# Putting the first chunk's residual into PSUM through TensorE, with ScalarE copying the sums out

## Chip, cores and metric

The kernel runs on one core of one Trainium2 chip. The metric is the device time of one execution in microseconds (us).

## The reference

Two layers, each a spectral mixing layer (A) and a feed-forward layer (B), both with a layer norm ahead and a residual addition behind:

```python
x = x + _A_ref(_layernorm(x, axis=-1), A_w_r, A_w_i)   # rfft2, times a filter, irfft2, to bf16
x = x + _B_ref(_layernorm(x, axis=-1), B_w1, B_b1, B_w2)
x = x + _A_ref(_layernorm(x, axis=-1), A_w_r, A_w_i)
x = x + _B_ref(_layernorm(x, axis=-1), B_w1, B_b1, B_w2)
# x: 1 x 2048 x 1024 bf16; B: 1024 -> 3584, h * tanh(softplus(h)), 3584 -> 1024
```

What matters here is the seam from A to B. It comes twice, near 110 and near 600 us.

## The kernel before

The residual stream lives in SBUF as `XS`, 16 tiles of 128 rows by 1024. At the seam the last stage of the inverse transform (`i4`) multiplies rows that come back from a round trip through HBM. The first chunk (tiles 0 to 3) is done in four quarters of 32 small products with 32 columns each; each quarter fills two PSUM banks. The other twelve tiles (the "remainder", 96 columns a product) follow in portions of 15 products between other work. While TensorE waits, `spin` gives it products that nobody reads, to keep its clock up.

```python
        self.spin(26, 0)                    # ahead of the wait for rows
# ...
    def i4(self, lo, nb, u0, n, bank):
        # ...
            fns.append(lambda e, l=l: e.matmul(self.PS[:, bank + l // k, l % k * w:(l % k + 1) * w], self.UT.ap[:, u0 + l, :],
                                               self.MT[:, 8 * lo:8 * lo + w], start=True, stop=True))
# ... i4_out, for the first chunk: VectorE adds the PSUM result to XS
                self.op(self.dve, lambda e, src=src, xs=xs: e.tensor_tensor(xs, src, xs, ALU.add), reads=rb, parts=self.r_xs[j])
# ... layer_B; rest(bank) is one portion of the remainder, copied out by ScalarE unless prog says otherwise
        for u in range(4):
            self.i4(0, 4, 32 * u, 32, 2 * u)
            self.i4_out(0, 4, 32 * u, 32, 2 * u, tiles=(0, 2))
            self.i4_out(0, 4, 32 * u, 32, 2 * u, staged=YC, tiles=(2, 2))
            for j in range(2):
                self.stats_quarter(j, u)    # VectorE, layer norm statistics
        rest(0)
        self.root(0, 2)                     # ScalarE square root, then VectorE reciprocal
        rest(3)
        for j in range(2):
            xn[j] = self.apply(j)           # VectorE normalises
        self.spin(6, 7)
        for j in range(2):
            transposed(0, j, xn[j])         # TensorE transposes, VectorE copies back
        rest(3)
        self.warm(ACT.Mish)
        # ... residual, statistics and apply of tiles 2 and 3
        for fg in range(4):
            mm1(0, fg, 0, mid=turns(0, 2, 3) if fg == 3 else ())   # first dense products
            rest(3)
            if fg == 2:
                rest(6, 10, dve)
        mm1(0, 0, 1)
        rest(3, 13)
```

## Time and profile before

| | before |
|---|---|
| time, median of the first three runs | 1017.54 us (1015.78 to 1019.77) |
| profiled execution, first to last instruction | 1016.2 us |
| mean granted TensorE clock of that execution | 0.998 |
| first seam: late rows land (116.31) to transposes (123.68) | 7.37 us |
| second seam: first small product (607.28) to transposes (616.01) | 8.73 us |
| either seam: transposes to first dense product | 2.00 us |
| either seam: first dense product to the gapless dense stretch | 14.56 us |

The last four rows are read off TensorE's line of the timeline. Its columns are start, duration, engine, line, operation, shapes, count, and in brackets how long the engine stood idle before and what ended that. First seam, kernel before:

```profile
116.31 3.21 PE L950 MATMUL PS<-MT,ARENA 128*128 128x32 bf16 x111 [0.94 <-DMA ARENA<-u_scratch]
120.07 0.81 PE L950 MATMUL PS<-MT,ARENA 128*128 128x96 bf16 x15 [0.55 <-ACT ARENA L550]
121.68 1.24 PE L628 MATMUL PS<-FD,BD 128*128 128x512 bf16 x5 [0.79 <-ACT ARENA L550]
123.68 1.08 PE L1006 MATMUL PS<-IDENT,ARENA 128*128 128x128 bf16 x16 [0.76 <-DVE ARENA L512]
...
125.68 1.92 PE L1040 MATMUL PS<-ARENA 128*128 128x256 bf16 x16 [0.29 <-DVE ARENA L1011]
```

The second seam, kernel before:

```profile
607.28 3.48 PE L950 MATMUL PS<-MT,ARENA 128*128 128x32 bf16 x128 [1.58 <-DMA ARENA<-u_scratch]
...
616.01 1.08 PE L1006 MATMUL PS<-IDENT,ARENA 128*128 128x128 bf16 x16 [0.76 <-DVE ARENA L512]
```

No hole of TensorE in the first seam, from the late rows on, is longer than 0.94 us: remainder products and the spin (L628) fill the time that VectorE takes. (The x111 of the first line holds the 96 late small products and the first remainder portion.) "Gapless" is the dense product (L1040) after the last remainder portion, at 140.24: from there on TensorE runs back to back.

### The profile page before, as it was taken

To read this page: it belongs to the slowest core of one execution; us is meant where nothing else is said; L and a number is where in the kernel's file an instruction comes from. 1 tells how busy PE (TensorE), PEld (TensorE's weight loads), DVE (VectorE), ACT (ScalarE), POOL (GpSimd) and SP (SyncE) were. 2 spreads that over 40 slices of the span, in tenths; PEclk is the share of its full clock that TensorE was granted. 3 is DMA by queue.
4 is the path that set the end of the run, shared out by engine and by line. 5 is a ranking of instruction groups with operands and counts; after the bars stand their busy time and mean duration, and the time that the engine had idled before them with its cause. 6 is when DMAs were issued, how large, how long until landed. Compare 5 with 4: busy or idle time off the path is not lost.

```text
span 1016.2 us, 13732 instructions
## 1 busy us (share of the span) xinstructions
PE 955.1 (94%) x5779; PEld 507.3 (50%) x5865; DVE 326.5 (32%) x679; ACT 347.3 (34%) x482; POOL 81.5 (8%) x114
## 2 busy tenths in 40 slices
PE   0799799999999999999999978999999999999998
PEld 0577575444444444444456757644444444444443
DVE  6797469002444000033347736830011100000111
ACT  7798384330000433300029847543100024330000
POOL 4651000000000000002511100000000000000000
PEclk9999999999999999999999999999999999999999
DMA  9979813562111220002932875246411212100000
GB/s 283 247 221 320 212 61 114 181 205 72 47 46 32 73 83 21 1 21 82 195 66 82 233 188 140 89 156 207 126 27 46 73 52 80 45 1 11 21 26 27
DMA packets 154205, 107.00 MB, mean 105 GB/s; under 512 B 74448, under 2 KB 133664, under 8 KB 154144
## 3 DMA queue, kind: packets, MB, share of 16 engines
q1 hardware_dynamic: 143056, 78.61, 27.3%
q0 software_dynamic: 8912, 25.84, 8.8%
q10 hardware_dynamic: 2176, 1.66, 0.5%
q8 instruction: 47, 0.77, 0.3%
q14 instruction: 14, 0.11, 0.0%
HBM read 80.85 MB, written 20.71 MB: 100 GB/s over the span
## 4 chain that ended last, share of the span: by engine, by line
PE 86%; DVE 4%; DMA 4%; ACT 4%; issue 1%; SPq 0%; POOL 0%; ACTq 0%; DVEq 0%; POOLq 0%
PE PS L1057 38%; PE PS L1040 37%; PE PS L771 2%; PE PS L697 2%; PE PS L792 2%; DMA ARENA<-c_bt 1%; PE PS L950 1%; ACT ARENA L441 1%; DMA ARENA<-u_scratch 1%; DVE ARENA L619 1%; DMA XS<-in_A_x_dram 1%; ACT ARENA L550 1%; PE PS L1006 1%; DVE ARENA L592 1%; PE PS L810 1%
## 5 line engine op out<-in xcount | busy, mean ns | idle before, releaser
L1040 PE MATMUL PS<-ARENA 128*128 128x512 bf16 (+1 forms) x1950 | 389.3, 358 | 2.5 <-DVE ARENA L1011 0.6
L1057 PE MATMUL PS<-ARENA 128*128 128x512 bf16 x1756 | 385.5, 379 | 1.9
L1044 ACT ACTIVATE ARENA<-PS,B 128x512 bf16<-128x512 f32 (+1 forms) x248 | 158.9, 645 | 410.9 <-PE PS L1040 410.6
L1040 PEld LDWEIGHTS PS<-ARENA 128*128 128x128 bf16 x1984 | 192.8, 98 | 193.8 <-DVE ARENA L1011 1.5
L1057 PEld LDWEIGHTS PS<-ARENA 128*128 128x128 bf16 x1792 | 175.4, 98 | 211.4
L1062 DVE TENSOR_TENSOR XS<-PS,XS 128x512 bf16<-128x512 f32 x64 | 44.2, 691 | 587.1 <-PE PS L1057 587.1
L460 DVE BATCH_NORM_STATS2 BN<-XS 128x6 f32<-128x512 bf16 x100 | 64.7, 675 | 6.2 <-DMA XS<-in_A_x_dram 5.0
L550 ACT ACTIVATE ARENA<-PS 128x1440 bf16<-128x1440 f32 (+3 forms) x26 | 28.0, 1095 | 28.0 <-DVE XS L972 24.4
L249 POOL DMA_DIRECT2D xn_scratch<-ARENA x12 | 6.5, 541 | 374.5 <-DVE ARENA L512 374.5
L771 PE MATMUL PS<-ARENA 128*128 128x256 bf16 x256 | 32.4, 273 | 4.1 <-DVE ARENA L760 3.2
L778 ACT ACTIVATE ARENA<-PS 128x1024 bf16<-128x1024 f32 x32 | 33.0, 1051 | 7.1 <-PE PS L771 7.1
L432 ACT ACTIVATE RS<-MV,EPS 128x2 f32<-128x2 f32 (+2 forms) x5 | 1.5, 298 | 96.8 <-DVE MV L463 96.2
L697 PE MATMUL PS<-FD,ARENA 128*128 128x256 bf16 (+1 forms) x256 | 31.8, 271 | 2.4 <-ACT ARENA L617 1.2
L749 ACT ACTIVATE ARENA<-PS 128x1024 bf16<-128x1024 f32 x32 | 32.5, 1044 | 4.5 <-PE PS L745 4.5
L771 PEld LDWEIGHTS PS<-ARENA 128*128 128x128 bf16 x256 | 24.2, 98 | 11.8 <-DVE ARENA L760 5.5
L753 DVE TENSOR_TENSOR ARENA<-ARENA 128x1024 bf16<-128x1024 bf16 x32 | 22.0, 688 | 20.4 <-ACT ARENA L749 20.3
L697 PEld LDWEIGHTS PS<-FD,ARENA 128*128 128x128 bf16 x256 | 24.4, 98 | 6.5 <-DVE ARENA L619 1.4
L820 ACT ACTIVATE ARENA<-PS 128x1024 bf16<-128x1024 f32 x26 | 26.7, 1063 | 2.4 <-PE PS L792 2.4
L792 PE MATMUL PS<-ARENA,BD 128*128 128x256 bf16 x192 | 24.9, 273 | 2.3 <-ACT ARENA L778 2.3
L950 PE MATMUL PS<-MT,ARENA 128*128 128x32 bf16 (+1 forms) x512 | 20.9, 195 | 4.5 <-DMA ARENA<-u_scratch 2.5
L512 DVE TENSOR_SCALAR ARENA<-XS,MV,RS 128x1024 bf16<-128x1024 bf16 x48 | 24.8, 542 | 1.0
L732 ACT ACTIVATE ARENA<-PS 128x1024 bf16<-128x1024 f32 x22 | 22.9, 1058 | 3.1 <-PE PS L697 3.1
(76 smaller groups left out, 515.5 us busy)
## 6 DMA issues: line engine op xcount, KB each, us to landing
ARENA<-in_B_w_dram SPq DMA_DIRECT2D x56, 512.0 KB, 3.9
ARENA<-in_B_w_dram SPq DMA_DIRECT2D x56, 256.0 KB, 4.1
u_scratch<-ARENA SPq DMA_DIRECT2D x14, 512.0 KB, 3.7
ARENA<-u_scratch SPq DMA_DIRECT2D x14, 512.0 KB, 6.1
w_scratch<-ARENA POOLq DMA_DIRECT2D x8, 512.0 KB, 6.2
ARENA<-w_scratch POOLq DMA_DIRECT2D x8, 512.0 KB, 5.4
out_dram<-XS SPq DMA_DIRECT2D x16, 256.0 KB, 2.0
ARENA<-xn_scratch POOLq DMA_DIRECT2D x15, 256.0 KB, 10.0
```

The source lines that it names most:

```text
L460: self.op(self.dve, lambda e: e.bn_stats(self.BN[:, j, 6 * h:6 * h + 6], self.XS[:, j, 512 * h:512 * h + 512]), reads=[self.r_xs[j]], part ...
L550: fn = (lambda e: e.activation(dst, src, ACT.Copy)) if scale is None else \
L697: fns.append(lambda e: e.matmul(dst, at(r), FD[:, t:t + n], start=start, stop=stop))
L749: self.op(act, lambda e: e.activation(x.ap.rearrange("p a b -> p (a b)"), ps, ACT.Copy, scale=SIG), reads=banks, writes=[x.res])
L771: fns.append(lambda e, c=c, part=part: e.matmul(ps[:, c * 256:(c + 1) * 256], yk.ap[:, part, c * P:(c + 1) * P], t[:, (128, 0)[part]:(384, ...
L778: self.op(act, lambda e: e.activation(v.ap[:, :, i, :], src, ACT.Copy), reads=banks, parts=[v.res])
L792: fns.append(lambda e, dst=dst, part=part, c=c: e.matmul(dst, BD[:, c:c + P], mov(kd, part), start=(part == 0), stop=(part == 1)))
L950: fns.append(lambda e, l=l: e.matmul(self.PS[:, bank + l // k, l % k * w:(l % k + 1) * w], self.UT.ap[:, u0 + l, :], self.MT[:, 8 * lo:8 * ...
L1040: fns.append(lambda e, db=db, bank=bank, fl=fl: e.matmul(PS[:, bank, 0:w], wb.ap[:, db, fl * P:(fl + 1) * P], x.ap[:, db, tok], start=(db ...
L1044: self.op(act, lambda e, bank=bank, ft=ft: e.activation(at.ap[:, ft, tok], PS[:, bank, 0:w], ACT.Mish, bias=self.B1[:, ft:ft + 1]), reads= ...
L1057: fns.append(lambda e, i=i, ft=ft: e.matmul(PS[:, bank, :], at.ap[:, ft, t * P:(t + 1) * P], W2[ft].ap[:, h * 512:(h + 1) * 512], start=(i ...
L1062: self.op(dve, lambda e: e.tensor_tensor(xs, PS[:, bank, :], xs, ALU.add), reads=[self.r_bank[bank]], writes=[self.r_xs[j]])
```

## The change

The intent is to take the residual addition from VectorE. During the wait for rows, eight identity products write `XS` into PSUM with `start=True`; the small products then accumulate on top; ScalarE copies finished sums out; VectorE only takes statistics. So 18 of 26 spin products go, as do the six behind. The root now stands ahead of the first remainder portion, the third remainder portion no longer stands between the transposes and the first dense product (two precede the transposes, as before), and the remainder's portions for VectorE move (10, 10 and 3 products for one of 10).

```diff
-        self.spin(26, 0)
+        self.spin(8, 0)
+        self.residual_first()
...
+    def residual_first(self):
+        for b in range(8):
+            out = self.PS[:, b, :].rearrange("p (l c) -> p c l", c=32)
+            xs = self.XS[:, 0:4, :].rearrange("p n (h l) -> p (n h) l", l=P)[:, :, 16 * b:16 * b + 16]
+            self.group([lambda e, out=out, xs=xs: e.matmul(out, self.IDENT[:], xs, start=True, stop=False)], ...)
...
-                                               self.MT[:, 8 * lo:8 * lo + w], start=True, stop=True))
+                                               self.MT[:, 8 * lo:8 * lo + w], start=lo > 0,
+                                               stop=lo > 0 or l % k == k - 1))
...
         for u in range(4):
             self.i4(0, 4, 32 * u, 32, 2 * u)
-            self.i4_out(0, 4, 32 * u, 32, 2 * u, tiles=(0, 2))
-            self.i4_out(0, 4, 32 * u, 32, 2 * u, staged=YC, tiles=(2, 2))
+            self.out_first(u, 0, act)
             for j in range(2):
                 self.stats_quarter(j, u)
+        for u in range(4):
+            self.out_first(u, 2, (act, act, act, dve)[u])
+        self.root(0, 2)
         rest(0)
-        self.root(0, 2)
         rest(3)
         for j in range(2):
             xn[j] = self.apply(j)
-        self.spin(6, 7)
         for j in range(2):
             transposed(0, j, xn[j])
-        rest(3)
         self.warm(ACT.Mish)
...
         for j in (2, 3):
-            residual(j)
             self.stats_dve(j)
...
             rest(3)
-            if fg == 2:
-                rest(6, 10, dve)
+            if fg:
+                rest(6, (10, 10, 3)[fg - 1], dve)
         mm1(0, 0, 1)
-        rest(3, 13)
+        rest(3)
```

More of the change, by code (lines that the diff above doesn't have):

```diff
@@ L942, in keep_filter @@
         self.dma(self.pool, self.w_d[g], self.wt_pair(i), f"ws{g % 4}", reads=[w.res for w in self.WT[i:i + 2]], writes=[self.r_wd[g]])
+    def residual_first(self):
+        for b in range(8):
+            out = self.PS[:, b, :].rearrange("p (l c) -> p c l", c=32)
+            xs = self.XS[:, 0:4, :].rearrange("p n (h l) -> p (n h) l", l=P)[:, :, 16 * b:16 * b + 16]
+            self.group([lambda e, out=out, xs=xs: e.matmul(out, self.IDENT[:], xs, start=True, stop=False)],
+                       reads=self.r_xs[0:4] + [self.r_ident], writes=[self.r_bank[b]])
+        for r in self.r_xs[0:4]:
+            r.begin()
     def i4(self, lo, nb, u0, n, bank):
@@ L950, in i4, with out_first, i4_out @@
             fns.append(lambda e, l=l: e.matmul(self.PS[:, bank + l // k, l % k * w:(l % k + 1) * w], self.UT.ap[:, u0 + l, :],
-                                               self.MT[:, 8 * lo:8 * lo + w], start=True, stop=True))
+                                               self.MT[:, 8 * lo:8 * lo + w], start=lo > 0,
+                                               stop=lo > 0 or l % k == k - 1))
         self.group(fns, reads=self.r_ut[u0 // 32:(u0 + n - 1) // 32 + 1] + [self.r_mt], writes=self.r_bank[bank:bank - (-n // k)])
-    def i4_out(self, lo, nb, u0, n, bank, staged=None, prog=None, tiles=None):
+    def out_first(self, u, t, prog):
+        b = slice(2 * u, 2 * u + 2)
+        src = self.PS[:, b, :].rearrange("p b (i c) -> p c b i", c=32)[:, 8 * t:8 * t + 16]
+        dst = self.XS[:, t:t + 2, :].rearrange("p n (h l) -> p (n h) l", l=P)[:, :, 32 * u:32 * u + 32]
+        self.copy(prog, dst.rearrange("p c (b i) -> p c b i", i=16), src, [], self.r_bank[b], parts=self.r_xs[t:t + 2])
+    def i4_out(self, lo, nb, u0, n, bank, staged, prog):
         w = 8 * nb
         k = 512 // w
-        t0, tn = tiles or (0, nb)
         for b0, m, i in ((0, n // k, k), (n // k, 1, n % k)):
@@ L962, in i4_out @@
                 continue
-            src = self.PS[:, bank + b0:bank + b0 + m, 0:i * w].rearrange("p b (i c) -> p c b i", c=w)[:, 8 * t0:8 * (t0 + tn)]
+            src = self.PS[:, bank + b0:bank + b0 + m, 0:i * w].rearrange("p b (i c) -> p c b i", c=w)
             l = slice(u0 + b0 * k, u0 + b0 * k + m * i)
-            rb = self.r_bank[bank + b0:bank + b0 + m]
-            def at(ap):
-                return ap.rearrange("p n (h l) -> p (n h) l", l=P)[:, :, l].rearrange("p c (b i) -> p c b i", i=i)
-            if staged is None:
-                j = slice(lo + t0, lo + t0 + tn)
-                xs = at(self.XS[:, j, :])
-                self.op(self.dve, lambda e, src=src, xs=xs: e.tensor_tensor(xs, src, xs, ALU.add), reads=rb, parts=self.r_xs[j])
-            else:
-                self.copy(prog or self.act, at(staged.ap), src, [], rb, parts=[staged.res])
+            dst = staged.ap.rearrange("p n (h l) -> p (n h) l", l=P)[:, :, l].rearrange("p c (b i) -> p c b i", i=i)
+            self.copy(prog, dst, src, [], self.r_bank[bank + b0:bank + b0 + m], parts=[staged.res])
     def load_w1(self, after=()):
@@ L1092, in layer_B @@
         YS.res.begin()
-        YC = self.alloc("YC", self.ob["XT1"], [2, self.D])
-        YC.res.begin()
         xn = {}
-        for j in range(2):
-            self.r_xs[j].begin()
         def at_tiles(c):
@@ L1114, in residual @@
         def residual(j):
-            y, i = (YS, j - 4) if j > 3 else (YC, j - 2)
-            self.op(dve, lambda e: e.tensor_tensor(self.XS[:, j, :], self.XS[:, j, :], y.ap[:, i, :], ALU.add),
-                    reads=[y.res], writes=[self.r_xs[j]])
+            self.op(dve, lambda e: e.tensor_tensor(self.XS[:, j, :], self.XS[:, j, :], YS.ap[:, j - 4, :], ALU.add),
+                    reads=[YS.res], writes=[self.r_xs[j]])
         def turns(c, *ts):
```

## The prediction

> **What bounds the kernel now.** I read first the page's busy shares, then its chain that ended last, then the chain of work in order of time, then groups by shape and the clock in short windows.
>
> ```profile
> PE 955.1 (94%) x5779; PEld 507.3 (50%) x5865; DVE 326.5 (32%) x679; ACT 347.3 (34%) x482; POOL 81.5 (8%) x114
> ...
> PE 86%; DVE 4%; DMA 4%; ACT 4%; issue 1%; SPq 0%; POOL 0%; ACTq 0%; DVEq 0%; POOLq 0%
> ```
>
> TensorE (PE) carries 86% of the chain that sets the end. The change doesn't touch its dense products (L1040, L1057); all it can win lies in the few per cent where the chain leaves TensorE. One such place comes twice, where each spectral layer ends and the feed-forward layer begins. The chain of work in order of time shows the first, from 107 to 124 us:
>
> ```profile
> 107.34 2.98 DMA u_scratch<-ARENA
> ...
> 111.69 4.58 DMA ARENA<-u_scratch
> 116.27 0.04 issue
> 116.31 0.98 PE PS L950 x32
> 117.30 0.02 issue
> 117.32 0.70 DVE XS L972
> 118.02 0.02 issue
> 118.04 0.75 DVE BN L472 x2
> 118.80 0.60 DVE XS L972
> 119.42 0.75 DVE BN L472 x2
> 120.18 0.60 DVE XS L972
> 120.80 1.86 ACT ARENA L550 x2
> 122.66 0.19 ACT RS L432
> ...
> 123.68 1.08 PE PS L1006 x16
> ```
>
> Columns: start, duration, what. A round trip through HBM (the wait for rows) ends at 116.27; then the small products L950 feed VectorE (DVE), which alternates the residual addition L972 and statistics L472, 1.35 us a turn, till ScalarE (ACT) takes the root and TensorE transposes at 123.68. The second occurrence has the same pieces, but all rows have landed when L950 starts at 607.28, and the transposes start at 616.01. There all four turns are bound by VectorE; in the first only the last three, as the rows of the second quarter came late.
>
> From the groups by shape between 100 and 186 us I take the costs:
>
> ```profile
> L628 PE MATMUL PS<-FD,BD 128*128 128x512 bf16 x30 | 6.8, 379 | 2.3 <-DVE ARENA L818 1.6 <-ACT ARENA L550 0.8
> ...
> L472 DVE BATCH_NORM_STATS2 BN<-XS 128x6 f32<-128x256 bf16 x8 | 3.1, 413 | 0.1
> ...
> L972 DVE TENSOR_TENSOR XS<-PS,XS 128x512 bf16<-128x512 f32 x4 | 2.7, 683 | 7.3 <-PE PS L950 7.3
> L550 ACT ACTIVATE ARENA<-PS 128x512 bf16<-128x512 f32 x4 | 2.4, 597 | 11.7 <-DVE XS L972 11.7
> ```
>
> L628 is the spin (products whose result nobody reads). L550 waited 11.7 us for L972: ScalarE stands idle beside a busy VectorE.
>
> **What the Trainium skill says.** "VectorE: DVE Perf Modes", section "The perf-mode tier table", has a two-tensor operation with a PSUM operand at its lowest rate; the trace agrees: 683 ns for 512 columns, where ScalarE copies the same 512 out in 597 ns. "PSUM — Partial Sum Buffer", section "The four PSUM rules", advises to "put any other seed through the PE (an identity matmul with `first_mm`)", which is what the change does, so accumulation should be right. Its section "Specifications" says that non-contiguous access to PSUM slows matmuls significantly. The new identity products write every 32nd column, so I expect them slower than the spin's; no matmul of the kernel before writes so, thus the trace can't say by how much. "TensorE: Matmul & The Clock Gate", Part 1, has the clock at half after an idle window of about 3.4 us. The trace shows a halving after less: TensorE idled 1.58 us before 607.28, and the windows read
>
> ```profile
> 607.20:608.20 1.00, 0.92 (x37) 0.95 (x38) 0.00 (x0) 0.00 (x0) 0.00 (x0) 1.00 0.42 63
> 608.20:609.20 1.00, 1.00 (x46) 1.00 (x43) 0.90 (x2) 0.20 (x1) 0.00 (x0) 0.78 0.00 0
> 609.20:610.20 1.00, 1.00 (x44) 1.00 (x41) 1.00 (x3) 0.39 (x1) 0.00 (x0) 0.50 0.15 37
> ```
>
> where the clock is the third number from the end. At the first occurrence it stays at 1.00.
>
> **The change part by part.** *During the wait* (108.79 to 114.41, and 600.14 to 607.28): 26 spin products in 5.56 us are 0.21 us each. Eight stay (1.7 us), and eight identity products come. At 0.21 each they take 1.7 us, at twice that 3.4, so that TensorE is done 3.4 to 5.1 us after the start, inside 5.6 and 7.1 us. Cost on the path: none, unless one takes over 0.5 us.
>
> *First occurrence.* Each quarter's L950 takes 0.98 us and the next follows, so the last ends at about 119.2. ScalarE copies tiles 0 and 1 of it by 119.85 (0.60). VectorE then has only the last statistics and aggregates, 1.30 us (120.80 to 122.10 before): 121.2. Before, the last addition ended at 120.77: 0.9 us won. ScalarE meanwhile takes three copies of tiles 2 and 3, each about 0.5 behind the one before: 121.4; the root follows to 121.6. VectorE does its one copy of the fourth quarter, about 0.68 (the 960-column copy takes 1.16, the 1024-column one 1.23, about 1 ns a column), till 121.9, then reciprocal and apply (0.18 and 0.56): transposes at 122.7 for 123.68, so **1.0 us won**.
>
> *Second occurrence.* All products are there (128 in 3.48 us, the last at 610.76). Last copy of tiles 0 and 1 at 611.4, statistics to 612.75 (before 614.43), VectorE's copy to 613.4, transposes at 614.25 for 616.01: **1.75 us won**.
>
> *Then the stretch to dense work* (first L1040 at 125.68 to the gapless stretch from 140.24, 14.56 us). The changed order does two of the twelve-tile remainders (L950, 15 columns each) ahead of the first L1040 instead of three, so the table load (1.28) and the first Mish follow two ScalarE copies of about 1.4 each: Mish can start at 125.85, not 128.51, some 1.1 us after the first L1040 (before 2.8). But 15 more columns fall into the stretch: at 0.043 us each 0.65 us of TensorE. The VectorE loses two additions L1116 (0.66 each) and gets copies of 10, 10 and 3 columns (1.16, 1.16, some 0.46) for one of 10. Replayed in program order with TensorE's start-to-start times (1.75 for 16 products of 256, 0.65 for 15 remainders, 0.9 for 16 transposes), ScalarE's 0.4 for a Mish and 1.4 for a remainder, I get three small stalls of together 0.5 us, against 1.3 before (0.58 at 130.65 for ScalarE, 0.38 at 135.53 for a copy are the largest). TensorE's work there was 5 × 1.75 + 83 × 0.043 + 0.9 = 13.25 us, of the 14.56; it becomes 13.9, and with 0.5 of stalls 14.4: **0.2 us won**. VectorE's first residual additions of tiles 4 to 7 come over a microsecond earlier too; the later stall for L1011 at 157.89 stays.
>
> Sum: (1.0 + 0.2) + (1.75 + 0.2) = 3.15 us, or 1014.4 from 1017.54. Everything after 140.24 is TensorE back to back and moves forward as it is.
>
> **The rivals.**
> *The clock takes the place of the wait.* The change removes 18 spin products ahead and 6 (1.24 us) behind, and with VectorE no longer slow TensorE has holes: at the second occurrence from 610.76 to about 612.5, until ScalarE has freed the banks for the remainder. Against it: the products after the wait ran 27 ns apart at clock 0.50 as at 1.00, so the small ones don't care. For it: remainders of 96 columns, transposes and L1040 do. A half-clock window of 3.4 us over them would cost 1 to 1.7 us at each occurrence; if at both, nothing is left of the gain: 1017 to 1018.
> *The identity products are slow.* At four times 0.21, eight take 6.8 us; with the spin 8.5 against 5.6 and 7.1 available: 1.6 us (first, counted from the second quarter 1.0) and 1.4 lost of the gain, 1016 to 1017. For it stands the skill's sentence; against it, that 18 spin products were taken away for 8, as if each were worth about two.
> *ScalarE becomes the bound.* It had 4.59 us of work in the 9.3 us from 114.3 to 123.6 and now takes all evacuations there but one. But it also takes none of the wait on L972 any more; its last copy ends 0.2 us after the statistics, but VectorE's own copy lasts until 0.3 us after the root and hides that. If the copies took 0.7 rather than 0.6 us, some 0.3 us would be lost each time: 1015.
> *More is won* if the stalls in the stretch vanish: 0.5 each time, 1013.3.
>
> **Range and chances.** I weigh the clock as likely at one of the two places (1 us) and take the prediction to 1015.2, 2.3 us below before. The three times before span 1015.78 to 1019.77, so a median strays by some 1 to 1.5 us by itself. Range 1012.4 to 1018.0. 2% are 20 us; from the landing of the rows to the gapless stretch there are 24 us (116.27 to 140.24) and 25 (607.28 to 632.57), of which TensorE works some 18 each, so at most 13 can be won in all: faster by over 2% gets 1%. Slower by over 2% would need a stall that nothing shows: 1%, and 98% for within.
>
> **What would show each step.** Identity products between 0.21 and 0.43 us apart, done before the first product after the wait. The transposes after apply start about 6.4 us after the late rows land in the first occurrence (before 123.68 − 116.27 = 7.4), and about 7.0 us after the first small product in the second (before 616.01 − 607.28 = 8.7). ScalarE waits for TensorE, no longer for VectorE, at its copies. First dense product (L1040) to the gapless stretch in about 14.4 us. Clock at 1.00 from 122 to 126 and from 612.5 to 616. The prediction is wrong if the small products start later than 5.6 and 7.1 us after the spin's start as before, if the clock reads 0.50 under L1040, or if the span falls by over 5 us.

## The result, and the profile after

| | before | after |
|---|---|---|
| median (range), four runs each | 1016.79 us (1015.78 to 1019.77) | 1015.41 us (1014.96 to 1016.21) |
| ratio, 95% interval | | 0.9982 (0.9959 to 1.0006) |
| profiled execution | 1016.2 us | 1013.1 us |
| its mean clock | 0.998 | 0.995 |

Ratios here are the mean time of one kernel's fast runs over the mean of the other's in the same rounds, so they are not quite the ratio of the medians. The result is correct, and inside 2%. The interval reaches past 1, so the timings alone do not show a gain. From the page after, the busy shares and the shares of the chain that ended last:

```profile
PE 952.0 (94%) x5749; PEld 506.0 (50%) x5833; DVE 323.9 (32%) x673; ACT 348.7 (34%) x484; POOL 81.6 (8%) x114
...
PE 87%; DMA 4%; SPq 3%; DVE 2%; ACT 2%; issue 1%; POOL 0%; ACTq 0%; DVEq 0%
```

TensorE still carries the chain; VectorE's and ScalarE's parts of it each fell from 4% to 2%. About half of each fall lies at the seams (100 to 142 and 590 to 634 us: VectorE 20.0 us of the chain before, 10.4 after; ScalarE 16.8 and 6.3), the other half ahead of 100 us, where nothing was changed. (Of the new 3% put down to a DMA queue, SPq, only some 1.2 us lie in each seam; the rest is elsewhere, where nothing was changed.) Of the 3.1 us between the two profiled executions, 1.6 lie ahead of the changed code: the last evacuation of the spectral layer, which both kernels have, ends at 108.51 before and at 106.90 after. So one may not read 3.1 us as the gain. TensorE's timeline of the first seam, after (L950 is now the identity product, L961 the small and the remainder products, L1016 the transposes, L1050 the first dense product):

```profile
108.92 3.61 PE L950 MATMUL PS<-XS,IDENT 128*128 128x512 bf16 x8
...
114.67 2.68 PE L961 MATMUL PS<-MT,ARENA 128*128 128x32 bf16 x96 [1.36 <-DMA ARENA<-u_scratch]
119.02 2.58 PE L961 MATMUL PS<-MT,ARENA 128*128 128x96 bf16 x30 [1.67 <-ACT XS L550]
121.40 1.40 PE L1016 MATMUL PS<-IDENT,ARENA 128*128 128x128 bf16 x16
123.74 1.92 PE L1050 MATMUL PS<-ARENA 128*128 128x256 bf16 x16 [0.94 <-DVE ARENA L1021]
...
131.94 1.04 PE L1050 MATMUL PS<-ARENA 128*128 128x256 bf16 x8
133.36 1.07 PE L1016 MATMUL PS<-IDENT,ARENA 128*128 128x128 bf16 x16 [0.38 <-DVE ARENA L554]
```

The identity products end before the late rows land (114.67). Transposes start 6.73 us after that, for 7.37. But there is a new hole: between the last small product and the first remainder TensorE is idle for 1.67 us, waiting for ScalarE to empty banks 0 to 2. The timeline of the other engines shows the rest of it:

```profile
117.39 2.06 ACT L550 ACTIVATE XS<-PS 128x512 bf16<-128x512 f32 x4 [0.26 <-PE PS L961]
...
119.37 0.29 ACT L432 ACTIVATE RS<-MV,EPS 128x2 f32<-128x2 f32 x1
...
119.98 1.00 DVE L512 TENSOR_SCALAR ARENA<-XS,MV,RS 128x1024 bf16<-128x1024 bf16 x2
```

ScalarE now follows TensorE, not VectorE. The first normalised tile is ready at about 120.5 (half of the 1.00 us after 119.98), yet its transposes start at 121.40: TensorE is still on the remainder, 30 products in 2.58 us, where the same 30 take 1.45 us in the second seam. The windows say why. Columns: window and length, busy time of TensorE, its weight loads, VectorE, ScalarE, GpSimd, then the granted clock, DMA share and GB/s:

```profile
116.80:117.60 0.80, 0.56 (x21) 0.45 (x17) 0.70 (x3) 0.54 (x2) 0.00 (x0) 0.50 1.00 284
117.60:118.40 0.80, 0.00 (x0) 0.00 (x0) 0.70 (x2) 0.80 (x3) 0.00 (x0) 0.50 1.15 344
...
120.00:120.80 0.80, 0.80 (x14) 0.80 (x12) 0.80 (x2) 0.36 (x1) 0.00 (x0) 0.50 1.12 285
```

The clock reads 0.50 from 115.2 to 122.2: it falls after the wait for rows (1.36 us) and stays down over the new hole. In the second seam of this trace it is at half only from 606.8 to 610.2, under small products; in a repeat it stays there until 614.0. Each first line below is the remainder, each second the transposes, second seam. This is the first trace after:

```profile
611.28 1.45 PE L961 MATMUL PS<-MT,ARENA 128*128 128x96 bf16 x30 [1.67 <-ACT XS L550]
612.84 1.08 PE L1016 MATMUL PS<-IDENT,ARENA 128*128 128x128 bf16 x16
```

and this the repeat (run after_again below):

```profile
611.19 2.58 PE L961 MATMUL PS<-MT,ARENA 128*128 128x96 bf16 x30 [1.67 <-ACT XS L550]
613.57 1.25 PE L1016 MATMUL PS<-IDENT,ARENA 128*128 128x128 bf16 x16
```

The same program lost a good microsecond to the clock in one and nothing in the other. The small products of the second seam after start at 605.73:

```profile
605.73 0.95 PE L961 MATMUL PS<-MT,ARENA 128*128 128x32 bf16 x32 [2.20 <-DMA ARENA<-u_scratch]
606.90 2.72 PE L961 MATMUL PS<-MT,ARENA 128*128 128x32 bf16 x96 [0.22 <-DMA ARENA<-u_scratch]
```

Stretch by stretch, in us from the traces:

| | before | after | after, repeat |
|---|---|---|---|
| 1st seam: late rows to transposes | 7.37 | 6.73 | 6.60 |
| transposes to first dense product | 2.00 | 2.34 | 2.35 |
| first dense product to gapless | 14.56 | 14.54 | 14.54 |
| 2nd seam: first small product to transposes | 8.73 | 7.11 | 7.56 |
| transposes to first dense product | 2.00 | 2.01 | 2.18 |
| first dense product to gapless | 14.56 | 14.54 | 14.54 |
| sum | 49.22 | 47.27 | 47.77 |

That is 1.95 and 1.45 us won, 0.19 and 0.14% of the span; the timed ratios say 0.18 and 0.14%, though with intervals of some ±0.2% that reach past 1.

These stretches leave the wait for rows out. Counted from the spectral layer's last evacuation to the gapless stretch, both seams together, the sums are 64.44 before, 62.86 after and 63.29 in the repeat: 1.58 and 1.15 us won. The difference is the second seam's rows, which landed later: the first small product starts 7.82 and 7.77 us after that evacuation, against 7.42 before. The identity products had ended by then (at 603.5), so they are not what it waited for.

### The profile page after: what moved, and what is told of

Same layout as the page of the kernel before. It is cut to its first block, busy times and chain, and to the rows that moved or that the text cites. A ratio compares the mean times of both kernels' runs of the same rounds, so it can differ in the third digit from the quotient of the medians.

```text
span 1013.1 us, 13670 instructions
## 1 busy us (share of the span) xinstructions
PE 952.0 (94%) x5749; PEld 506.0 (50%) x5833; DVE 323.9 (32%) x673; ACT 348.7 (34%) x484; POOL 81.6 (8%) x114
## 4 chain that ended last, share of the span: by engine, by line
PE 87%; DMA 4%; SPq 3%; DVE 2%; ACT 2%; issue 1%; POOL 0%; ACTq 0%; DVEq 0%
PE PS L1067 38%; PE PS L1050 38%; SPq L249 3%; PE PS L771 2%; PE PS L697 2%; PE PS L792 2%; PE PS L961 2%; DMA ARENA<-in_A_w_i_dram 1%; DMA ARENA<-u_scratch 1%; DMA ARENA<-c_bt 1%; DMA u_scratch<-ARENA 1%; PE PS L1016 1%; PE PS L743 1%; ACT ARENA L778 1%; PE PS L810 1%
## 5 line engine op out<-in xcount | busy, mean ns | idle before, releaser
L1050 PE MATMUL PS<-ARENA 128*128 128x512 bf16 (+1 forms) x1950 | 389.1, 358 | 3.8 <-DVE ARENA L1021 1.9
L1050 PEld LDWEIGHTS PS<-ARENA 128*128 128x128 bf16 x1984 | 193.0, 98 | 194.7 <-DVE ARENA L1021 2.9
L961 PE MATMUL PS<-MT,ARENA 128*128 128x32 bf16 (+1 forms) x512 | 21.4, 199 | 7.1 <-DMA ARENA<-u_scratch 3.8
L961 PEld LDWEIGHTS PS<-MT,ARENA 128*128 128x128 bf16 x512 | 20.0, 102 | 9.8 <-issue 4.5
```

What stands on the lines that cost most here:

```text
L1050: fns.append(lambda e, db=db, bank=bank, fl=fl: e.matmul(PS[:, bank, 0:w], wb.ap[:, db, fl * P:(fl + 1) * P], x.ap[:, db, tok], start=(db ...
```

## The experiments

Theory: the gain is VectorE's relief at the seam, less what the clock takes back where removed spin and new holes drop it. Rival: the gain comes from what else the diff does (root ahead of the remainder, no portion between transposes and first dense product), and VectorE's addition matters little. Edits are against the kernel after unless a line says otherwise.

**A repeat, and the spin ahead of the wait.** The repeat is the kernel after as it is.

> The changed kernel once more, unedited, for a second trace and a tighter ratio. Stretch = from the first spin product after the spectral layer to the first dense product of the gapless stretch (31.45 and 32.43 us in the trace of the kernel before, 31.10 and 31.20 in that of the changed one, so 1.58 us won in sum). Theory (the change wins 1 to 2 us, the rest of the 3.1 us between the two profiled spans came before the changed code): ratio 0.998 to 0.999; stretches within 0.5 us of 31.10 and 31.20 if the clock falls in the same places. Rival (all 3.1 us are the change's): ratio 0.997. If the half-clock time is a matter of a window that doesn't start with the kernel, the mean clock differs between the timed runs (0.993 to 0.996 seen so far) and the place of the half clock differs between the traces.

Ratio 0.9986 (0.9968 to 1.0004), median 1015.77 over six runs (1014.26 to 1020.19). The same size of gain, and again an interval that reaches past 1. Of the two stretches that the expectation names, the first is as said (31.19), the second is not (32.00 for 31.20): the clock fell elsewhere, as seen above.

```diff
-        self.spin(8, 0)
+        self.spin(12, 0)     # spin12;  spin0: line removed
```

> Twelve spin products ahead of the identity products instead of eight: 0.85 us more TensorE work inside the wait. Clock theory (the half clock from 115.4 to 122 us in the changed kernel's first occurrence comes of the holes in TensorE's work that the removed spins left, and costs 0.5 to 1 us there): clock stays at 1.00 in the first occurrence, the 30 remainder products ahead of the transposes take about 1.45 us instead of 2.58, first stretch 30.3 to 30.7 instead of 31.10, ratio to before about 0.9975. Rival (the half clock is chance, or caused by the later hole while ScalarE empties banks): the half clock is there as before and the stretch stays at 31.1.

> No spin products at all ahead of the identity products: 1.7 us less TensorE work inside the wait. Clock theory: half clock in both occurrences, reaching under the remainders and transposes in at least one; stretches (from the first identity product, so 1.7 us shorter by definition; compare by the landing of the rows) lengthen by 0 to 1 us each, mean clock lower than with eight, ratio 0.9985 to 1.000. Rival (spins don't matter): ratio as that of the changed kernel, mean clock as well.

spin12: 0.9981 (0.9966 to 0.9995). spin0: 0.9982 (0.9967 to 0.9996). More spin ahead did not keep the clock (first seam at half from 120.8 to 124.2, second from 609.0 to 615.8), and none at all lowered the mean clock of the runs to 0.990 to 0.995 without costing time. So **the amount of spin ahead of the wait made no difference that these runs can tell** (some ±0.15%). What follows the wait first are small products, which hardly feel the clock: in the second seam before they start 25 ns apart at full clock, up to 608.77, and 27 ns at half.

**How much an identity product costs, and why.** The first variant puts the stride on the read from SBUF instead of on the write to PSUM; the second has no stride at all and computes something else (relative error 0.71). Its output is wrong, which doesn't matter for the time.

```diff
# sbuf_stride
-            out = self.PS[:, b, :].rearrange("p (l c) -> p c l", c=32)
-            xs = self.XS[:, 0:4, :].rearrange("p n (h l) -> p (n h) l", l=P)[:, :, 16 * b:16 * b + 16]
+            out = self.PS[:, b, :].rearrange("p (l c) -> p l c", c=32)
+            xs = self.XS[:, 0:4, :].rearrange("p n (h l) -> p l (n h)", l=P)[:, 16 * b:16 * b + 16, :]
# contig_wrong
+            out = self.PS[:, b, :]
+            xs = self.XS[:, b // 2, 512 * (b % 2):512 * (b % 2) + 512]
```

> The identity products read with the stride (one bf16 every 256 bytes of SBUF) and write PSUM without one; same result. In the changed kernel they are 0.428 us apart, twice the spin's 0.21, with the stride on the writing side. If the PSUM stride is what doubles them, and a strided read costs nothing: 0.21 us apart. If a strided read costs as much: 0.43 again. If the layout is not the cause at all (a wait or weight load for each): 0.43 again with weight loads as late as now, 0.29 us of idle before each. The end moves by nothing either way, as the products end inside the wait for rows.

> Wrong result on purpose: the identity products read and write without a stride. They are 0.428 us apart in the changed kernel with the stride in PSUM, and 0.86 with the stride in SBUF. If strides alone are the cause: 0.21 to 0.22 apart, as the spin. If each product's own wait and signal cost something: more than 0.25. The time is about that of the changed kernel, as the products end inside the wait for rows in all three but the one with the stride in SBUF.

The line of the identity products by itself (minimum, median and maximum of the duration in ns), first of the kernel after, then of sbuf_stride, then of contig_wrong:

```profile
L950 PE MATMUL PS<-XS,IDENT x16: 602/634/634, 108.9 to 602.9; 128*128 128x512 bf16 x16
```

```profile
L950 PE MATMUL PS<-XS,IDENT x16: 1017/1036/1037, 110.9 to 608.7; 128*128 128x512 bf16 x16
```

```profile
L950 PE MATMUL PS<-XS,IDENT x16: 379/379/390, 111.2 to 603.5; 128*128 128x512 bf16 x16
```

Start to start, eight of them are 0.43, 0.86 and 0.22 us apart (for the kernel after: 3.61 less the last one's 0.63, over 7). So the product that writes every 32nd fp32 column of PSUM costs twice a plain one, and the one that reads every 128th bf16 element of SBUF four times. (The first also reads in runs of 16 columns, which contig_wrong changes too; the two were not separated.) sbuf_stride, one run at 1020.86 us, is correct; its identity products end after the rows have landed, and its first small product starts 8.86 us after the spectral layer's last evacuation instead of 5.42. I had expected its end not to move: a miss, as I had not expected the SBUF stride to cost more than the PSUM one.

**Each half of the change alone.** psum_only keeps the residual in PSUM and goes back to the old order of root and portions; order_only keeps VectorE's additions and takes the new order (against the kernel before). Neither has the six spin products.

```diff
# psum_only
-        self.root(0, 2)
         rest(0)
+        self.root(0, 2)
         rest(3)
@@ after the transposes
+        rest(3)
@@ and the tail
-            if fg:
-                rest(6, (10, 10, 3)[fg - 1], dve)
+            if fg == 2:
+                rest(6, 10, dve)
-        rest(3)
+        rest(3, 13)
# order_only, against before
+        self.root(0, 2)
         rest(0)
-        self.root(0, 2)
@@
-        self.spin(6, 7)
@@ after the transposes
-        rest(3)
@@ and the tail as in the kernel after
```

> The residual through PSUM and the copies by ScalarE as changed, but the remainders in the order of the kernel before (three ahead of the table load, VectorE takes ten columns once), the spin ahead of the transposes left out. Theory (the gain comes from VectorE no longer adding): nearly all of the gain is here: transposes 0.7 to 1.2 us earlier than before in each occurrence, from the first dense product to the gapless stretch 14.5 us as before, ratio 0.998 to 0.9985. Rival (the new order of the remainders brings the gain): stretches as before, ratio 1.000.

> The kernel before with only the new order: root ahead of the remainders, two remainders instead of three ahead of the table load, VectorE copies out 10, 10 and 3 columns, no spin ahead of the transposes; the residual still added by VectorE. Times from the end of the last spectral eviction (before: transposes at 15.17 and 16.15, gapless dense products at 31.73 and 32.71). Theory, after the run with the PSUM part alone was 3 us slower: the root waits for statistics alone instead of for a remainder's copy, 0.4 us earlier each time; transposes 14.8 and 15.7, gapless 31.3 and 32.3, ratio 0.9990 to 0.9995, so that about half of the change's gain is the order's and the PSUM part needs the order. Rival (the order is worth nothing without the PSUM part): gapless as before, ratio 1.000. Mean clock 0.998 as before if the holes come of the PSUM part, 0.996 or less if they come of the missing spin ahead of the transposes.

psum_only: 1.0031 (1.0019 to 1.0043), median 1021.05. order_only: 1.0034 (1.0021 to 1.0048), median 1021.25. **Each half alone, without the six spin products, makes the kernel slower**, against my expectations. In psum_only ScalarE, in program order, first copies the remainder and then takes the root for which everybody waits (first seam):

```profile
121.88 1.37 ACT L550 ACTIVATE ARENA<-PS 128x1440 bf16<-128x1440 f32 x1 [0.41 <-PE PS L961]
123.15 0.29 ACT L432 ACTIVATE RS<-MV,EPS 128x2 f32<-128x2 f32 x1
```

The statistics were done near 121.3, so the root is about 1.8 us late; then the half clock lies under transposes and first dense products (123.2 to 130.0; 16 dense products took 3.33 us instead of 1.92). In order_only the order is good, but without the six spin products TensorE stands idle for 2.39 us and meets the dense products at half clock:

```profile
123.61 1.08 PE L1006 MATMUL PS<-IDENT,ARENA 128*128 128x128 bf16 x16 [2.39 <-DVE ARENA L512]
125.61 3.45 PE L1040 MATMUL PS<-ARENA 128*128 128x256 bf16 x16 [0.93 <-DVE ARENA L1011]
```

**Each half again, with spin.** order_spin is order_only with `self.spin(6, 7)` kept. psum_root has the PSUM part, root first, three spin products ahead of the transposes, and otherwise the old order.

```diff
# order_spin, against order_only
+        self.spin(6, 7)
         for j in range(2):
             transposed(0, j, xn[j])
# psum_root, against psum_only
+        self.root(0, 2)
         rest(0)
-        self.root(0, 2)
@@
+        self.spin(3, 7)
         for j in range(2):
             transposed(0, j, xn[j])
```

> The order alone again (residual still added by VectorE), but with the six spin products ahead of the transposes kept. The order alone without them was 0.34% slower at a mean clock of 0.990 to 0.993. Clock theory (the missing spin, not the order, made it slow): half clock no longer under the first dense products, first dense to gapless 14.5 us (without the spin 16.1 and 16.8), from the end of the last spectral eviction transposes at 14.4 to 14.8 and 15.0 to 15.7, mean clock 0.998, ratio 0.9985 to 0.9995. Rival (the order itself, with two more copies by VectorE, makes it slow): ratio 1.002 or more as without.

> The residual through PSUM with the remainders as before (three ahead of the table load, VectorE ten columns once), but the root ahead of the first remainder, and three spin products ahead of the transposes. With the remainder ahead of the root it was 0.31% slower. Theory (there ScalarE's copy of the remainder, 1.4 us, stood between the statistics and the root): root at 12.3 and 13.3 us after the last spectral eviction (not 15.0 and 15.2), transposes at 14.4 and 15.3, gapless at 31.0 to 31.3 and 31.9 to 32.2, ratio 0.998 to 0.999, as the whole change. Rival (two remainders ahead of the table load and the columns for VectorE are needed for the gain): ratio 0.9995 or more.

order_spin: 0.9979 (0.9964 to 0.9993), median 1015.85; clock 0.998 to 1.000 in all five runs. First seam:

```profile
120.62 1.47 PE L628 MATMUL PS<-FD,BD 128*128 128x512 bf16 x6 [0.57 <-ACT ARENA L550]
...
124.44 1.92 PE L1040 MATMUL PS<-ARENA 128*128 128x256 bf16 x16 [0.93 <-DVE ARENA L1011]
```

Six spin products turn order_only's mean of 1021.72 us into 1016.24, and the same 16 dense products take 1.92 us again. So the order with the spin kept, and with **VectorE adding as before**, is by its timing as fast as the whole change. psum_root: 0.9993 (0.998 to 1.0006), median 1017.39: the PSUM part with the root first and otherwise the old order is not told from before. The interval covers both what the theory expected (0.998 to 0.999) and what the rival did, so this run decides nothing; and as it adds the root and the spin at once, it does not say which of the two psum_only lacked.

One caution. order_spin's stretches sum to 6.97 + 2.00 + 14.75 + 8.32 + 2.01 + 14.74 = 48.79 us, only 0.43 less than before, while its timed gain is 2.1 us (interval 0.7 to 3.7). Part of the time came from elsewhere: in its trace the rows of the second seam land 5.94 us after the spectral layer's last evacuation, before it was 7.42. No part of the edit reaches the transfers ahead; order_only, which lacks only the spin, has 6.69. One trace of each can't tell luck from effect.

**The stall in the middle of the dense products.** Tiles 2 and 3 are transposed in the fourth dense group, and their bank waits for a VectorE copy (0.38 us, in the timeline after). turn3 makes that copy small:

```diff
-                rest(6, (10, 10, 3)[fg - 1], dve)
+                rest(6, (10, 3, 10)[fg - 1], dve)
```

> The changed kernel with VectorE's columns 10, 3, 10 instead of 10, 10, 3 and nothing else. If the stall of 0.38 us ahead of the transposes of tiles 2 and 3 comes of VectorE's second copy of ten columns: from first dense to gapless 14.0 instead of 14.54 in both occurrences, ratio 0.997 to 0.998. If the better time of the version with one copy for each quarter and spins came of this alone, the ratio is 0.996 here too; if of the clock, the mean clock here stays at 0.991 to 0.997 and the time about 2 us above that version's.

Ratio 0.9962 (0.9948 to 0.9976), median 1014.59. First dense product to gapless: 13.99 and 13.98 us for 14.54, and in the first seam the transposes follow without a wait:

```profile
132.12 1.07 PE L1016 MATMUL PS<-IDENT,ARENA 128*128 128x128 bf16 x16
```

That is 1.1 us shown in the trace; the timed difference to the kernel after is about twice that, with intervals that overlap.

**The hole ahead of the remainder, and the clock by itself.** onecopy lets ScalarE copy all four tiles of a quarter at once, so a bank pair is free after one copy; with it one remainder portion goes ahead of the root, and the (10, 3, 10) of turn3. onecopy_spin differs only by seven spin products ahead of the transposes.

```diff
# onecopy
-        src = self.PS[:, b, :].rearrange("p b (i c) -> p c b i", c=32)[:, 8 * t:8 * t + 16]
-        dst = self.XS[:, t:t + 2, :]...
+        src = self.PS[:, b, :].rearrange("p b (i c) -> p c b i", c=32)
+        dst = self.XS[:, 0:4, :]...
@@
-        for u in range(4):
-            self.out_first(u, 2, (act, act, act, dve)[u])
-        self.root(0, 2)
         rest(0)
+        self.root(0, 2)
@@ and (10, 3, 10)
# onecopy_spin, against onecopy
+        self.spin(7, 7)
         for j in range(2):
             transposed(0, j, xn[j])
```

> The changed kernel, but ScalarE copies all four tiles of a quarter in one instruction of 1024 columns (1.05 us for 0.60 + 0.60), so that banks 0 to 2 are free as soon as the last small products end; VectorE copies nothing; remainder ahead of the root again; VectorE's columns are 10, 3, 10 instead of 10, 10, 3. Theory (hole of 1.67 us in TensorE while ScalarE empties banks): that hole is gone, remainders start 0.1 us after the small products. From the end of the last spectral eviction: transposes at 13.6 to 14.0 and 14.6 to 15.0 (changed kernel 14.35 to 14.5 and 14.9 to 15.3); from first dense to gapless 14.15 instead of 14.54, as the stall of 0.38 us ahead of the transposes of tiles 2 and 3 goes; sum of the stretches 61.2 to 62.2 (changed kernel 62.9 and 63.3), ratio 0.997. Rival (ScalarE is the bound: longer copies delay the statistics as much): transposes as in the changed kernel, gain only 0.4 us each from the stall.

> The same with seven spin products (1.5 us) between the remainders and the transposes. Clock theory: without them TensorE has a hole of about 2 us there and the clock is at half under the transposes or the first dense products in some executions; with them transposes take 1.08 us and not 1.4 to 1.8, mean clock of the timed runs is up by 0.001 to 0.003, 0.3 to 0.8 us better than without in each occurrence. Rival (the half clock comes of the small products themselves[...]): mean clock and stretches as without.

onecopy: 1.0009 (0.9993 to 1.0024), median 1019.15, clocks 0.990 to 0.997. The hole is gone (126 small and remainder products from 116.74 without a wait), yet the expected 0.997 was missed. onecopy_spin: **0.9960 (0.9947 to 0.9972)**, median 1013.92, clocks 0.997 and 0.998 in all five runs. TensorE in the first seam, onecopy first:

```profile
123.09 1.08 PE L1016 MATMUL PS<-IDENT,ARENA 128*128 128x128 bf16 x16 [2.39 <-DVE ARENA L512]
125.09 3.31 PE L1050 MATMUL PS<-ARENA 128*128 128x256 bf16 x16 [0.93 <-DVE ARENA L1021]
```

```profile
120.81 1.68 PE L628 MATMUL PS<-FD,BD 128*128 128x512 bf16 x7
123.26 1.07 PE L1016 MATMUL PS<-IDENT,ARENA 128*128 128x128 bf16 x16 [0.77 <-DVE ARENA L512]
125.26 1.92 PE L1050 MATMUL PS<-ARENA 128*128 128x256 bf16 x16 [0.93 <-DVE ARENA L1021]
```

Work that computes nothing, 1.68 us of it at this seam and all inside a wait, shortens the kernel by 4.6 us (mean 1018.71 to 1014.11). The pair differs in nothing else. The trace of onecopy, one of its two fastest runs (1016.73 us), shows 1.4 us of it, at the first seam's dense products; where the slower runs lose the rest was not traced. onecopy_spin and turn3 are the fastest versions found, both faster than the kernels before and after by the medians; between the two this can't decide.

## Why the prediction was right

The predicted 1015.2 us met 1015.41, and the class with it. That they meet within 0.2 us is partly luck: the kernel before alone spans 4 us, and the terms of the sum did not all come out. By its steps:

- **Identity products: right.** Said to be 0.21 to 0.43 us apart and inside the wait; measured 0.43, done at 112.5 with the late rows at 114.67. The rival that they cost four times 0.21 didn't come true for the PSUM stride; it did for the SBUF stride (0.86), and cost what that rival says.
- **First seam: right in direction, mis-sized.** Transposes were to come 6.4 us after the late rows; they came after 6.73 and 6.60, so 0.6 to 0.8 us were won and not 1.0. The normalised tile was even earlier than worked out (about 5.8 us after the rows), but the remainder at half clock held TensorE until 6.73. A cost that the sum lacked: the transposes, too, ran at half clock, so that the first dense product follows after 2.34 us instead of 2.00.
- **Second seam: right.** 7.0 us from first small product to transposes predicted, 7.11 and 7.56 measured, 1.6 and 1.2 us won of 1.75. The difference of the two, 0.45, is 0.82 us of the clock under the remainder, less 0.37 by which the remainder started later in the first trace, where the later quarters' rows came late. One sign of being wrong did come true: the small products started 7.54 us after the spin's first record (repeat 7.72), later than the 7.1 named. But they waited for rows, not for the identity products.
- **First dense product to gapless: mis-sized.** 14.4 predicted, 14.54 measured: 0.02 us won each time and not 0.2. turn3, without a stall, takes 13.99. So TensorE's work there is 13.99 where I replayed 13.9, and the stalls are 0.55 for 0.5.
- **The clock takes the place of the wait: this rival came true**, at one of the two seams in the first trace and at both in the repeat. I had put it at about 1 us at one seam. (That small products run 27 ns apart at both clocks was misread: 25 at full, 27 at half. The conclusion stands.) What I had named as the danger, half clock under the dense products, did not happen in the kernel after, where the remainder sits between hole and dense work and takes the slow time; it did happen in psum_only, order_only and onecopy, all of which are slower than or no faster than before.
- **ScalarE becomes the bound: in part.** Its copies are 0.60 us as said, and the hole of 1.67 us is its emptying of the banks for the remainder. The normalised tile was not late for it.

What the prediction did not see is **how much the order and the spin are worth**. It credits VectorE's relief. By the timings, the order with the old additions and the old spin behind gives 0.9979, and the PSUM part with the root first 0.9993. The stretches are kinder to the prediction: to the transposes order_spin wins 0.40 and 0.41 us, the kernel after 0.64 and 1.62 (repeat 0.77 and 1.17). So VectorE's relief is there, but its share of the timed gain is not shown. What the PSUM part is worth depends on the spin: order_only has neither, and from there (1.0034) adding the PSUM part leads to the kernel after (0.9982 and 0.9986), while adding six spin products leads to the same place (0.9979). As the traces read, both do it in the same way: they put work of TensorE into the time ahead of the transposes (the remainder at 119.02 in the kernel after, the spin at 120.62 in order_spin), so that the half clock doesn't reach the dense products.

Open: why order_spin's timed gain is larger than its stretches show; how much of onecopy_spin's lead over order_spin (0.9960 to 0.9979) is the PSUM part and how much (10, 3, 10), as order_spin with (10, 3, 10) was not run; which part of the new order counts; and how fast the kernel after is with its six spin products kept, which was not run either.

On what drops the clock the traces say more, though no run tested it. In each trace half clock begins and ends on one grid of 3.41 us (in the kernel after at 115.30, 122.12, 606.82 and 610.23). Count how much of each grid interval TensorE's columns fill, from 100 to 150 and from 590 to 640 us, at 216 ns for 512 columns as the spin takes them, and twice that for the strided identity products. In the 13 traces other than sbuf_stride's, all 25 intervals at full clock with 36% or less are followed by half clock, and none of the 320 with 37.5% or more. (sbuf_stride's four falls fit only if its identity products count once and not by their 0.86 us.) Small products, 32 columns every 25 ns, fill about half of their time by this count, so that in psum_root 1.1 us without work behind them was enough (34%).

## What to carry to other kernels

Ahead of dense products, a hole in TensorE can cost more than the wait itself (here some 1.5 us where 16 dense products ran at half clock): fill it with throwaway products placed right before the dense work, and look at the clock column under the products that follow, not at the mean. Where a change bundles a new mechanism with a new order of instructions, run the order by itself with everything else kept: here it is, by the timings, worth as much as the whole. An in-order engine that stands between statistics and root should take the root before any bulk copy (the root came 1.8 us late in psum_only).

## What the Trainium skill lacked or had wrong

- "PSUM — Partial Sum Buffer", section "Specifications", says that non-contiguous access slows matmuls significantly, without a size. Here a 512-column product that writes every 32nd fp32 column took 0.43 us start to start against 0.22 contiguous: twice (with its reads in runs of 16 columns, not separated).
- "SBUF — State Buffer", section "Door 1: The DMA port swizzle (why `[64,N]` ≈ `[32,N]`)", says that reads which leave a 16-byte line pay a penalty, without a size for an operand of a product. Here reading every 128th bf16 element took 0.86 us, four times contiguous and twice the PSUM stride, so moving the stride from PSUM to SBUF is the wrong way.
- "TensorE: Matmul & The Clock Gate", Part 1, has the half clock after an idle window of about 3.4 us that runs freely. The unit agrees (half from 606.8 to 610.2 in the kernel after, 119.8 to 123.2 in psum_root), and so does that the same program meets it differently from run to run. But no window here was idle throughout: holes of 2.39 us, with work on either side (ending at 123.61 in order_only, at 123.09 in onecopy), were followed by half clock, from 125.4 and from 124.6. The page gives no share of a window that is enough; here the line lies between 36 and 37.5% filled, by the count above.
